# Gated linear attention with a gated feed-forward layer: PSUM banks split two for the late attention units and three in turn for gate, value and unit outputs, gating ranked first in the planner from step 15, last output banks finished one after another

## The chip, the cores and the metric

The kernel runs on one core of a Trainium2 chip. The metric is device time in microseconds (us). Three runs of the kernel before gave 572.51, 572.71 and 572.79 us, median 572.71. A profile of one more execution gives every number of the trace that follows.

The core's engines have queues of their own and run them in order: TensorE (PE: matmuls, with its weight loads shown as PEld), VectorE (DVE), ScalarE (ACT), GpSimd (POOL) and SyncE (SP, which here only issues DMAs). They wait for each other through semaphores.

## The reference

```python
def _attn_ref(q, k, v, alpha):                    # (4, 8, 768, 48) each
    B, H, S, D = q.shape
    state = np.zeros((B, H, D, D), dtype=np.float32)
    y = np.zeros_like(q)
    for t in range(S):
        state = alpha[:, :, t, :, None] * state + np.einsum('bhd,bhe->bhde', k[:, :, t], v[:, :, t])
        y[:, :, t] = np.einsum('bhd,bhde->bhe', q[:, :, t], state)
    return y.astype(np.float32)

def _moe_ref(x, w_gate, w_val, w_out):            # x (3072, 384), d_ff 1536
    gate = 1.0 / (1.0 + np.exp(-(x @ w_gate)))
    val = x @ w_val
    return (gate * val @ w_out).astype(np.float32)
```

The attention's output, laid out as 3072 tokens of 384 channels, is the x of the feed-forward layer. The weights are fp32, and the gate's weights are drawn larger by a factor of 6.92.

## The kernel before

**The feed-forward part: 72 steps.** The tokens are cut into six groups of 512, and d_ff into 12 blocks of 128. Step s works on group s // 12 and block s % 12. Every fp32 factor is split into a high and a low part, and a product is formed from three of the four partial products (`PAIRS`), so a step has 27 matmuls of 128x512: nine for the gate into bank `pg` and nine for the value into bank `pv` (`products`, L221), and nine into the three output banks `po0` to `po2` (`back`, L607). Between them stands the gating: the sigmoid `sg` on ACT (L594), `pv` times `sg` in place on DVE (L596), its high part `hh` cast on ACT (L598), and its low part `hl` by a subtraction on DVE (L599). Two of the three output partial products need `hh` alone, the third needs `hl`. `sg` has one buffer, `hh` and `hl` two. After a group's last step the three output banks are copied to SBUF (L620 on DVE, L622 on ACT) and sent out by SP (L623).

**The attention part: 24 units**, four for each group, each for two heads and 512 tokens. Units 0 to 7 come first (`unit`); units 8 to 23 (`late`) are spread over the steps, one in three, so that unit u's outputs follow steps 13, 16, ... 58. On the way a late unit goes through: loads of its rows (L498 to L509), a backward scan `G` on DVE (L366), the keys times `G` on POOL (L373), a forward scan `F` on DVE (L370), the queries times `F` on DVE (L514, two halves into the buffer `A`), four transposes on PE (L385) and their copy `kn` on ACT (L389), sixteen-fold small matmuls for the scores (L525) and for the state increments (L532), eight recurrent state updates `st` on DVE (L551), four masked copies of the scores on DVE (L538), the states times the decay on POOL (`vs`, L556), and the outputs on PE (L568). The outputs are split into `yt`, the high part on ACT (L396) and the low part on DVE (L397), and SP moves them into x (L405), from which the next group's steps read.

**The eight PSUM banks** are: three called `at` (`r_at`), one `pg`, one `pv`, three `po`. A late unit takes the three `at` banks for its transposes (`pk`) and for scores and increments (`pas[0]`, `pas[1]`). Its outputs go into the bank `pg`, the one that every step's gate uses too.

**What sets the order.** Nothing is issued where it stands in the code. Each piece is handed to `Plan.add` with its engine, an estimate of its duration, a key (the step at which it is due) and what it reads and writes. `Plan.order` first works out for each piece how late it may end (`latest`, from its key and from its users), then plays the engines forward with the estimated durations, and each time takes, of the pieces of an engine that could begin, the one with the smallest `latest`. The queues that result are fixed in the program: each engine then runs its queue in order, whatever the true durations are. Parts that share a PSUM bank or an SBUF buffer wait for each other through semaphores.

**The end.** The last step's pieces are keyed half a step earlier. After the plan, each engine loads a flag (`found`) and branches past a fallback loop (`general`) that the inputs here do not take.

The lines that set the places named here:

```python
r_bank = Ring([*r_at.tiles, *r_po.tiles, *r_pg.tiles])          # units 0 to 3
(pkn, pk), *pas = r_at.next(), r_at.next(), r_at.next()         # L517, late units
pyn, py = r_pg.tiles[0]                                         # L562, a late unit's outputs
n = min((n for n in ns if begin[n] <= t + 1e-9), key=lambda n: (latest[n], n))   # L108
```

Of the kernel before, what the change touches and what calls it, by code (L numbers as in the profile page):

```python
# [17 lines left out]
P = 128  # L18
# [30 lines left out]
class Plan:  # L49
# [14 lines left out]
    def add(self, engine, time, key, fn, reads=(), writes=(), port=False, fixed=False):  # L64
# [12 lines left out]
        self.parts.append((engine, time, key, fn, deps, port or engine == "gpsimd", fixed))  # L77

    def order(self):
# [14 lines left out]
        for n in reversed(range(len(self.parts))):  # L94
# [4 lines left out]
            latest[n] = by if key is None else key * self.STEP if self.parts[n][6] and key > NF + 2 else min(by, key * self.STEP)  # L99
        begun, memory, port, busy = [None] * len(self.parts), 0.0, 0.0, {}  # L100
        for _ in self.parts:
            best = None
            for e, ns in waiting.items():
# [4 lines left out]
                n = min((n for n in ns if begin[n] <= t + 1e-9), key=lambda n: (latest[n], n))  # L108
# [88 lines left out]
def gla_then_glu(ctx: ExitStack, tc: tile.TileContext, q, k, v, alpha, rows, vc, vh, weights_in, out):  # L197
# [11 lines left out]
    found = nc.values_load(within[0:1, 0:1], min_val=0, max_val=1)  # L209
# [15 lines left out]
def chunked(ctx, tc, rows, vc, vh, weights_in, out, const, ident, flags, weights, within):  # L225
# [70 lines left out]
    r_bank = Ring([*r_at.tiles, *r_po.tiles, *r_pg.tiles])  # L296
    ob = [(f"raw{i // 2}", raws[i // 2][1].rearrange("p a b -> p (a b)").bitcast(F32)[:, i % 2 * T:(i % 2 + 1) * T]) for i in range(NM)]
# [196 lines left out]
    def late(u, g, p, t):  # L494
# [22 lines left out]
        (pkn, pk), *pas = r_at.next(), r_at.next(), r_at.next()  # L517
# [44 lines left out]
        pyn, py = r_pg.tiles[0]  # L562
# [20 lines left out]
    def step(s):  # L583
        g, f = divmod(s, NF)
        got = {}
        for nm, r, dt in (("g", r_pg, 0.0), ("v", r_pv, 0.33)):
            pn, pt = r.next()
            got[nm] = (pn, pt)
            for tiles in ([range(NK - 1), range(NK - 1, NK)] if s < 2 else [range(NK)]):
                plan.add("tensor", (MM * 3 * len(tiles), 1.0), s + dt, lambda nm=nm, pt=pt, tiles=tiles: products(  # L590
                    nc, pt[:, 0:T], lambda a, i: weights.part(nm, a, f)[:, i], lambda b, i: xin(g)[:, i, b, :], tiles),
                    [*weight(nm, f), *(x for x in xparts[g] if x[1] in tiles)], [pn])
        (sgn, sg), (hhn, hh), (hln, hl) = r_sg.next(), r_hh.next(), r_hl.next()
        plan.add("scalar", act(T), None, lambda: nc.scalar.activation(out=sg, in_=got["g"][1][:, 0:T], func=AF.Sigmoid), [got["g"][0]], [sgn])  # L594
        pvn, pv = got["v"][0], got["v"][1][:, 0:T]
        plan.add("vector", vec(T), None, lambda: nc.vector.tensor_tensor(out=pv, in0=pv, in1=sg, op=ALU.mult), [sgn], [pvn])  # L596
        last = s == NG * NF - 1
        plan.add("scalar", act(T), None, lambda: nc.scalar.copy(out=hh, in_=pv), [pvn], [hhn])  # L598
        plan.add("vector", vec(T), None, lambda: nc.vector.tensor_tensor(out=hl, in0=pv, in1=hh, op=ALU.subtract), [pvn, hhn], [hln])  # L599
# [224 lines left out]
```

## Time and profile before

The profiled execution took 573.94 us; from its first to its last instruction is a span of 572.2 us, and the mean granted TensorE clock is 0.991. It lies 1.2 us above the median of the runs.

| stretch (us) | what runs | PE busy | DVE busy | PE clock |
|---|---|---|---|---|
| 28.6 to 57.2 | first units, first steps | 24.05 of 28.60 | 24.12 | 0.88 |
| 178.62 to 463.03 | thirteen periods of three steps and one late unit | 280.57 of 284.41 | 172.27 | 1.00 |
| 483 to 560 | steps alone | 77.00 of 77.00 | 17.44 | 1.00 |

Over the span PE is busy for 96%, DVE for 60%, ACT for 32% and POOL for 18%. A row of the timeline gives start, duration, engine, line, operation, output <- inputs, shape and count, and in brackets how long the engine was idle before it and what ended that. Matmuls overlap: a 128x512 matmul is shown with some 0.40 us, while the next one begins 0.23 us after it, so the time that PE loses is read from start to start rather than from the busy share.

### The profile page before, as it was taken

The page shows a single profiled execution, that of the slowest core. Times are in us where ns is not written, and L with a number is a line of the kernel's source. Part 1 is how long each engine was busy: PE and PEld are TensorE (multiplying, and loading weights), DVE is VectorE, ACT ScalarE, POOL GpSimd, SP SyncE. Part 2 cuts the span into 40 slices and gives each one's busy share as a digit, 9 for nine tenths or more (in the row PEclk, how much of TensorE's full clock was granted, in tenths as well). Part 3 has the DMA queues.
Part 4 walks back from the last instruction along what each step waited for, and adds up shares of the span by engine and source line. Part 5 has one row for each costly group of instructions (what it writes and reads, how often), then busy time and mean ns, then how long its engine had stood idle before and what let it go on. Part 6 is the DMA issues. An engine that isn't in the chain of part 4 may idle for free.

```text
span 572.2 us, 10280 instructions
## 1 busy us (share of the span) xinstructions
PE 550.2 (96%) x4150; PEld 434.2 (76%) x4150; DVE 344.9 (60%) x648; ACT 183.4 (32%) x331; POOL 102.2 (18%) x133
## 2 busy tenths in 40 slices
PE   8979999989999999999999999999999999999995
PEld 4657887767787787877877877877877878888783
DVE  7797989899848457467466476476475242311221
ACT  1557667653222222322222321321321222212111
POOL 7531212132202112112022022022021010000000
PEclk9988999999999999999999999999999999999998
DMA  8764765634414214314123224034131011100001
GB/s 327 239 189 152 256 209 177 196 122 124 136 32 113 75 37 111 125 42 113 52 61 111 85 82 112 13 100 112 58 109 49 13 29 29 56 0 1 1 0 62
DMA packets 21833, 55.93 MB, mean 98 GB/s; under 512 B 3472, under 2 KB 8592, under 8 KB 21776
## 3 DMA queue, kind: packets, MB, share of 16 engines
q1 hardware_dynamic: 21776, 55.17, 31.7%
q8 instruction: 35, 0.57, 0.4%
q14 instruction: 22, 0.18, 0.1%
HBM read 41.01 MB, written 4.72 MB: 80 GB/s over the span
## 4 chain that ended last, share of the span: by engine, by line
PE 76%; DVE 15%; issue 3%; DMA 2%; POOL 1%; SPq 1%; ACT 0%; DVEq 0%; POOLq 0%; ACTq 0%
PE pg L221 26%; PE pv L221 25%; PE po L607 17%; DVE st L551 6%; DVE A L538 4%; DVE yt L397 2%; PE at L525 2%; PE at L385 1%; DMA x<-yt 1%; PE pv L579 1%; PE at L532 1%; PE at L437 1%; POOL in L425 1%; DVE w L340 1%; POOL in L373 1%
## 5 line engine op out<-in xcount | busy, mean ns | idle before, releaser
L221 PE MATMUL pg<-x,w 128*128 128x512 f32 x648 | 163.6, 396 | 7.0 <-DVE yt L397 4.3
L221 PE MATMUL pv<-x,w 128*128 128x512 f32 x648 | 161.8, 394 | 1.0 <-DVE hl L599 1.0
L596 DVE TENSOR_TENSOR pv<-pv,sg 128x512 f32<-128x512 f32 x72 | 50.3, 699 | 175.5 <-PE pv L221 175.5
L221 PEld LDWEIGHTS pg<-x,w 128*128 128x128 f32 x648 | 120.2, 188 | 40.4 <-DVE yt L397 10.9
L221 PEld LDWEIGHTS pv<-x,w 128*128 128x128 f32 x648 | 120.6, 188 | 26.7 <-DVE hl L599 1.5
L607 PE MATMUL po<-hh,w 128*128 128x512 f32 x432 | 116.2, 401 | 1.2 <-ACT hh L598 1.2
L594 ACT ACTIVATE sg<-pg 128x512 f32<-128x512 f32 x72 | 43.1, 599 | 175.8 <-PE pg L221 175.7
L607 PEld LDWEIGHTS po<-hh,w 128*128 128x128 f32 x432 | 79.4, 188 | 20.6 <-ACT hh L598 1.5
L598 ACT CAST hh<-pv 128x512 fp32r<-128x512 f32 x72 | 42.2, 587 | 121.3 <-DVE pv L596 121.2
L556 POOL TENSOR_TENSOR vs<-st,dec 64x384 f32<-64x384 f32 x32 | 26.8, 839 | 226.1 <-DVE st L551 224.9
L607 PE MATMUL po<-hl,w 128*128 128x512 f32 x216 | 63.3, 399 | 0.0
L599 DVE TENSOR_TENSOR hl<-pv,hh 128x512 fp32r<-128x512 f32 x72 | 49.2, 683 | 20.5 <-ACT hh L598 20.4
L373 POOL TENSOR_TENSOR in<-in,G 128x512 f32<-128x512 f32 x22 | 33.9, 1541 | 86.6 <-DVE G L366 45.2
L607 PEld LDWEIGHTS po<-hl,w 128*128 128x128 f32 x216 | 40.4, 188 | 9.7 <-issue 0.2
L551 DVE SCALAR_TENSOR_TENSOR st<-st,dec,at 128x48 f32<-128x48 f32 x128 | 33.9, 265 | 9.4 <-PE at L532 4.1
L514 DVE TENSOR_TENSOR A<-A,F 64x512 f32<-64x512 f32 x32 | 33.4, 1043 | 0.5
L366 DVE TENSOR_TENSOR_SCAN G<-in,d1g 128x512 f32<-128x512 f32 x22 | 27.8, 1262 | 2.0 <-DMA in<-in_rows_dram 2.0
L370 DVE TENSOR_TENSOR_SCAN F<-in,d1f 128x512 f32<-128x512 f32 x22 | 28.7, 1304 | 0.0
L538 DVE TENSOR_TENSOR A<-at,mask 64x256 f32<-64x256 f32 x64 | 27.0, 422 | 1.1
L378 ACT ACTIVATE F<-F 128x512 f32<-128x512 f32 x23 | 14.5, 631 | 22.7 <-DVE A L514 16.9
L336 DVE SCALAR_TENSOR_TENSOR raw<-raw 128x576 uint32<-128x576 uint32 (+1 forms) x28 | 20.5, 751 | 0.8 <-ACT raw L333 0.8
L389 ACT COPY kn<-at 128x512 f32<-128x512 f32 x22 | 12.9, 584 | 15.5 <-PE at L385 15.5
(132 smaller groups left out, 400.1 us busy)
## 6 DMA issues: line engine op xcount, KB each, us to landing
in<-in_rows_dram SPq DMA_DIRECT2D x16, 516.5 KB, 3.9
raw<-in_w_dram SPq DMA_DIRECT2D x12, 576.0 KB, 4.9
x<-yt SPq DMA_DIRECT2D x35, 192.0 KB, 3.4
first_w<-in_w_dram SPq DMA_DIRECT2D x10, 576.0 KB, 4.5
out_dram<-raw SPq DMA_DIRECT2D x18, 256.0 KB, 2.4
v<-in_vc_dram SPq DMA_DIRECT2D x22, 192.0 KB, 4.8
A<-in_rows_dram SPq DMA_DIRECT2D x32, 128.0 KB, 4.1
in<-in_rows_dram SPq DMA_DIRECT2D x4, 772.5 KB, 5.2
```

The lines of the kernel that those rows point to most:

```text
L221: nc.tensor.matmul(out=dst, lhsT=lhs(a, i), rhs=rhs(b, i), start=(n == 0 and i == 0), stop=(n == len(todo) - 1 and i == NK - 1))
L366: plan.add("vector", scan(n), t["G"], lambda: nc.vector.tensor_tensor_scan(out=G[:, ::-1], data0=az[:, n:0:-1], data1=d1g[size], initial=0 ...
L370: plan.add("vector", scan(n), after(t["G"], 0.01), lambda: nc.vector.tensor_tensor_scan(out=F, data0=az[:, 0:n], data1=d1f, initial=0.0, o ...
L373: plan.add("gpsimd", pool_(n), t["kt"], lambda: nc.gpsimd.tensor_tensor(out=kT, in0=kT, in1=G, op=ALU.mult), [gn, (inn, "r")], [(inn, "k")])
L514: plan.add("vector", vec(T), t["q"], lambda j=j: nc.vector.tensor_tensor(out=A[own[j], j], in0=A[own[j], j], in1=F[own[j]], op=ALU.mult), ...
L538: plan.add("vector", vec(T // 2), t["mask"], lambda pa=pa, j=j, i=i: nc.vector.tensor_tensor(out=A[other[j], j].rearrange("p (c i t) -> p ...
L551: nc.vector.scalar_tensor_tensor(out=st[:, c + 1, :], in0=st[:, c, :], scalar=dec[:, c:c + 1], in1=pas[c % 2][1][:, T // 2 + c // 2 * D:T ...
L594: plan.add("scalar", act(T), None, lambda: nc.scalar.activation(out=sg, in_=got["g"][1][:, 0:T], func=AF.Sigmoid), [got["g"][0]], [sgn])
L596: plan.add("vector", vec(T), None, lambda: nc.vector.tensor_tensor(out=pv, in0=pv, in1=sg, op=ALU.mult), [sgn], [pvn])
L598: plan.add("scalar", act(T), None, lambda: nc.scalar.copy(out=hh, in_=pv), [pvn], [hhn])
L599: plan.add("vector", vec(T), None, lambda: nc.vector.tensor_tensor(out=hl, in0=pv, in1=hh, op=ALU.subtract), [pvn, hhn], [hln])
L607: nc.tensor.matmul(out=pso_now[m][1][:, 0:T], lhsT=weights.part("o", b, f)[:, m * P:(m + 1) * P], rhs=h[a][:, 0:T], start=(f == 0 and i == ...
```

## The change

It has five parts:

1. **Banks.** Two rings are added over banks that exist already. Late units take their three banks from `r_two` (`at0`, `at1`), so that `pk` and `pas[1]` are one bank. From step 12 the gate, the value and a late unit's outputs take the next bank of `r_three` (`pg`, `pv`, `at2`), in the order in which the code names them.
2. **Rank.** From step 15 the four gating pieces (`sg`, the product in place, `hh`, `hl`) carry `soon`, which puts them ahead of every other piece of their engine that could begin at the same time. Their `latest` is unchanged.
3. **The last step's output matmuls** are keyed bank by bank (all three products of `po0`, then of `po1`, then of `po2`) instead of product by product.
4. **The last output bank** `po2` is copied in two halves, columns 0 to 255 on ACT and 256 to 511 on DVE; the banks before it and all earlier groups are copied whole as before.
5. The flag `found` is loaded inside the `with` that holds the fast path's pools instead of just behind it.

```diff
-    def add(self, engine, time, key, fn, reads=(), writes=(), port=False, fixed=False):
+    def add(self, engine, time, key, fn, reads=(), writes=(), port=False, fixed=False, soon=False):
...
+        rank = [t - 1000.0 if p[7] else t for t, p in zip(latest, self.parts)]
...
-                n = min((n for n in ns if begin[n] <= t + 1e-9), key=lambda n: (latest[n], n))
+                n = min((n for n in ns if begin[n] <= t + 1e-9), key=lambda n: (rank[n], n))
...
-    found = nc.values_load(within[0:1, 0:1], min_val=0, max_val=1)
+        found = nc.values_load(within[0:1, 0:1], min_val=0, max_val=1)
...
+    r_two, r_three = Ring(r_at.tiles[:2]), Ring([*r_pg.tiles, *r_pv.tiles, r_at.tiles[2]])
...
-        (pkn, pk), *pas = r_at.next(), r_at.next(), r_at.next()
+        (pkn, pk), *pas = r_two.next(), r_two.next(), r_two.next()
...
-        pyn, py = r_pg.tiles[0]
+        pyn, py = r_three.next()
...
-            pn, pt = r.next()
+            pn, pt = (r_three if g else r).next()
...
+        soon = s > NF + 2
...
-        plan.add("scalar", act(T), None, lambda: nc.scalar.activation(out=sg, in_=got["g"][1][:, 0:T], func=AF.Sigmoid), [got["g"][0]], [sgn])
+        plan.add("scalar", act(T), None, lambda: nc.scalar.activation(out=sg, in_=got["g"][1][:, 0:T], func=AF.Sigmoid), [got["g"][0]], [sgn], soon=soon)
...
-                plan.add("tensor", (MM * len(some), 1.0), s + 1 + 0.66 + 0.01 * m + 0.1 * some[0] - (0.5 if last else 0), lambda m=m, some=some: back(m, some),
+                plan.add("tensor", (MM * len(some), 1.0), s + 1 + 0.66 + (0.1 * m + 0.01 * some[0] - 0.5 if last else 0.01 * m + 0.1 * some[0]), lambda m=m, some=some: back(m, some),
...
+                for half in range(2):
+                    cs = slice(half * T // 2, (half + 1) * T // 2) if last and m == NM - 1 else slice(0, T)
+                    n = cs.stop - cs.start
+                    if n == T and half != m % 2:
+                        continue
+                    if half:
+                        plan.add("vector", vec(n), s + 1.9, lambda pt=pt, to=to, cs=cs: nc.vector.tensor_copy(out=to[:, cs], in_=pt[:, cs]), [pn], [("ob", m, half), *over])
+                    else:
+                        plan.add("scalar", act(n), s + 1.9, lambda pt=pt, to=to, cs=cs: nc.scalar.copy(out=to[:, cs], in_=pt[:, cs]), [pn], [("ob", m, half), *over])
```

The other three gating pieces get `soon=soon` in the same way. Lines move by three to nine: L607 becomes L611, L568 L571, L385 L388, L397 L400, L599 L603, L620 L629.

PE's queue is the same up to step 10. In the steady part it reads so behind the outputs of the late unit that follow step 22, before (the number behind a name is the buffer's: `at2_119` is the third `at` bank, `x1_653` the next group's x, `w10` the weights of block 10):

```order
L568 MATMUL pg0_120<-A1_87,vs1_89 48x64 x16
L607 MATMUL po0_122<-hh1_114,w9_1037 128x512 x2
...
L607 MATMUL po0_122<-hl1_116,w9_1037 128x512
...
L607 MATMUL po0_122<-hh0_113,w10_1127 128x512 x2
...
L221 MATMUL pg0_120<-x0_111,w11_1250 128x512 x9
L221 MATMUL pv0_121<-x0_111,w11_1250 128x512 x9
L607 MATMUL po0_122<-hl0_115,w10_1127 128x512
...
L221 MATMUL pg0_120<-x1_653,w0_429 128x512 x9
L385 MATMUL at0_117<-ident_58,in1_79 128x128 x4
L221 MATMUL pv0_121<-x1_653,w0_429 128x512 x9
```

And with the change (of the three `po` banks only the first one's rows are shown, here and above):

```order
L571 MATMUL at2_119<-A1_87,vs1_89 48x64 x16
L611 MATMUL po0_122<-hh1_114,w9_1037 128x512 x2
...
L611 MATMUL po0_122<-hl1_116,w9_1037 128x512
...
L222 MATMUL pg0_120<-x0_111,w11_1250 128x512 x9
L222 MATMUL pv0_121<-x0_111,w11_1250 128x512 x9
L611 MATMUL po0_122<-hh0_113,w10_1127 128x512 x2
...
L611 MATMUL po0_122<-hl0_115,w10_1127 128x512
...
L222 MATMUL at2_119<-x1_653,w0_429 128x512 x9
L222 MATMUL pg0_120<-x1_653,w0_429 128x512 x9
L388 MATMUL at1_118<-ident_58,in1_79 128x128 x4
```

The outputs go into a bank that the next gate does not use; the six `hh` matmuls of block 10 that stood ahead of that gate now stand behind its value product, and the transposes stand behind a value product instead of between gate and value. The next group's first gate comes 36 matmuls after the outputs (9 output, 18 gate and value, 9 output) where it came 36 after them as well (15, 18 and 3).

DVE's queue at the same place, from the last state update on, before:

```order
L551 SCALAR_TENSOR_TENSOR st1_108<-st1_108,dec1_97,at2_119 128x48
L538 TENSOR_TENSOR A1_87<-at1_118,mask64_104 64x4x64
L538 TENSOR_TENSOR A1_87<-at2_119,mask64_104 64x4x64
...
L397 TENSOR_TENSOR yt0_85<-pg0_120,yt0_85 128x512
L599 TENSOR_TENSOR hl1_116<-pv0_121,hh1_114 128x512
L366 SCALAR_TENSOR_TENSOR G1_91<-in1_79,d1g64_102 128x512
L514 TENSOR_TENSOR A0_86<-A0_86,F0_92 64x512 x2
...
L596 TENSOR_TENSOR pv0_121<-pv0_121,sg0_112 128x512
```

And with the change (the two masked copies stand twice in each queue, the small pieces of 8 columns are left out):

```order
L554 SCALAR_TENSOR_TENSOR st1_108<-st1_108,dec1_97,at1_118 128x48
L603 TENSOR_TENSOR hl1_116<-pv0_121,hh1_114 128x512
L541 TENSOR_TENSOR A1_87<-at0_117,mask64_104 64x4x64
L541 TENSOR_TENSOR A1_87<-at1_118,mask64_104 64x4x64
...
L400 TENSOR_TENSOR yt0_85<-at2_119,yt0_85 128x512
L369 SCALAR_TENSOR_TENSOR G1_91<-in1_79,d1g64_102 128x512
L517 TENSOR_TENSOR A0_86<-A0_86,F0_92 64x512
L600 TENSOR_TENSOR pv0_121<-pv0_121,sg0_112 128x512
L517 TENSOR_TENSOR A0_86<-A0_86,F0_92 64x512
```

`hl` moves ahead of the masked copies and of `yt`; the next step's product goes between the two halves of the queries' multiplication.

Where the change to the rank begins, PE's queue of steps 10 to 13 differs by more than this. Behind the six output matmuls of block 10 it has, before and then with the change (rows of the other `po` banks left out):

```order
L385 MATMUL at0_117<-ident_58,in1_79 128x128 x4
L221 MATMUL pv0_121<-x0_111,w11_1250 128x512 x9
L221 MATMUL pg0_120<-x1_653,w0_429 128x512 x9
L607 MATMUL po0_122<-hl0_115,w10_1127 128x512
...
L607 MATMUL po0_122<-hh1_114,w11_1250 128x512 x2
L221 MATMUL pg0_120<-x1_653,w1_496 128x512 x9
L221 MATMUL pv0_121<-x1_653,w0_429 128x512 x9
```

```order
L222 MATMUL pv0_121<-x0_111,w11_1250 128x512 x9
L222 MATMUL pg0_120<-x1_653,w0_429 128x512 x9
L611 MATMUL po0_122<-hl0_115,w10_1127 128x512
...
L388 MATMUL at1_118<-ident_58,in1_79 128x128 x4
L611 MATMUL po0_122<-hh1_114,w11_1250 128x512 x2
L222 MATMUL pv0_121<-x1_653,w0_429 128x512 x9
```

The transposes move from before block 11's value product to behind the next gate. At the very end, DVE's half of the last bank waits in the built program for ACT's half of the same bank; the two do not run side by side.

More of the change, by code (lines that the diff above doesn't have):

```diff
@@ L76, in add @@
         deps.discard(n)
-        self.parts.append((engine, time, key, fn, deps, port or engine == "gpsimd", fixed))
+        self.parts.append((engine, time, key, fn, deps, port or engine == "gpsimd", fixed, soon))
     def order(self):
@@ L592, in step @@
                     [*weight(nm, f), *(x for x in xparts[g] if x[1] in tiles)], [pn])
+        soon = s > NF + 2
         (sgn, sg), (hhn, hh), (hln, hl) = r_sg.next(), r_hh.next(), r_hl.next()
-        plan.add("scalar", act(T), None, lambda: nc.scalar.activation(out=sg, in_=got["g"][1][:, 0:T], func=AF.Sigmoid), [got["g"][0]], [sgn])
+        plan.add("scalar", act(T), None, lambda: nc.scalar.activation(out=sg, in_=got["g"][1][:, 0:T], func=AF.Sigmoid), [got["g"][0]], [sgn], soon=soon)
         pvn, pv = got["v"][0], got["v"][1][:, 0:T]
-        plan.add("vector", vec(T), None, lambda: nc.vector.tensor_tensor(out=pv, in0=pv, in1=sg, op=ALU.mult), [sgn], [pvn])
+        plan.add("vector", vec(T), None, lambda: nc.vector.tensor_tensor(out=pv, in0=pv, in1=sg, op=ALU.mult), [sgn], [pvn], soon=soon)
         last = s == NG * NF - 1
-        plan.add("scalar", act(T), None, lambda: nc.scalar.copy(out=hh, in_=pv), [pvn], [hhn])
-        plan.add("vector", vec(T), None, lambda: nc.vector.tensor_tensor(out=hl, in0=pv, in1=hh, op=ALU.subtract), [pvn, hhn], [hln])
+        plan.add("scalar", act(T), None, lambda: nc.scalar.copy(out=hh, in_=pv), [pvn], [hhn], soon=soon)
+        plan.add("vector", vec(T), None, lambda: nc.vector.tensor_tensor(out=hl, in0=pv, in1=hh, op=ALU.subtract), [pvn, hhn], [hln], soon=soon)
         h = (hh, hl)
@@ L618, in step @@
                 over = [(on, "u"), (on, "l")] if g == 0 else []
-                if m % 2:
-                    plan.add("vector", vec(T), s + 1.9, lambda pt=pt, to=to: nc.vector.tensor_copy(out=to, in_=pt[:, 0:T]), [pn], [("ob", m), *over])
-                else:
-                    plan.add("scalar", act(T), s + 1.9, lambda pt=pt, to=to: nc.scalar.copy(out=to, in_=pt[:, 0:T]), [pn], [("ob", m), *over])
+                for half in range(2):
[7 more added lines that the diff above has]
+                        plan.add("scalar", act(n), s + 1.9, lambda pt=pt, to=to, cs=cs: nc.scalar.copy(out=to[:, cs], in_=pt[:, cs]), [pn], [("ob", m, half), *over])
                 plan.add("sync", (0.475, 1.0), s + 1.9, lambda to=to, m=m: nc.sync.dma_start(
-                    out=out[m * P:(m + 1) * P, g * T:(g + 1) * T], in_=to), [("ob", m)])
+                    out=out[m * P:(m + 1) * P, g * T:(g + 1) * T], in_=to), [("ob", m, 0), ("ob", m, 1)])
     pso = []
```

## The prediction

> **What bounds the kernel now.** I read the page's chain first, then the table of who waited for whom, then the timeline of one period of three steps in the steady part.
>
> ```profile
> PE 76%; DVE 15%; issue 3%; DMA 2%; POOL 1%; SPq 1%; ACT 0%; DVEq 0%; POOLq 0%; ACTq 0%
> L221 PE MATMUL pg<-x,w 128*128 128x512 f32 x648 | 163.6, 396 | 7.0 <-DVE yt L397 4.3
> PE pg L221 <- DVE yt L397: 4.3, 15, 0.6
> ```
>
> The chain that ended last is mostly PE. PE's largest wait on another engine, in total, is that of the gate's matmuls for `yt`: fifteen times, 4.3 us. One period shows what stands behind it (PE alone):
>
> ```profile
> 222.33 2.34 PE L221 MATMUL pg<-x,w 128*128 128x512 f32 x9 [0.27 <-DVE yt L397]
> 224.51 2.20 PE L221 MATMUL pv<-x,w 128*128 128x512 f32 x9
> 227.25 2.21 PE L221 MATMUL pg<-x,w 128*128 128x512 f32 x9
> 229.31 0.60 PE L385 MATMUL at<-ident,in 128*128 128x128 f32 x4
> 229.66 2.32 PE L221 MATMUL pv<-x,w 128*128 128x512 f32 x9
> 231.82 1.57 PE L607 MATMUL po<-hh,w 128*128 128x512 f32 x6
> 233.23 0.87 PE L607 MATMUL po<-hl,w 128*128 128x512 f32 x3
> 233.93 2.24 PE L221 MATMUL pg<-x,w 128*128 128x512 f32 x9
> 236.01 2.20 PE L221 MATMUL pv<-x,w 128*128 128x512 f32 x9
> ...
> 239.13 1.10 PE L568 MATMUL pg<-A,vs 128*48 128x64 f32 x32
> 240.16 1.67 PE L607 MATMUL po<-hh,w 128*128 128x512 f32 x6
> 242.37 1.56 PE L607 MATMUL po<-hh,w 128*128 128x512 f32 x6
> 244.20 2.11 PE L221 MATMUL pg<-x,w 128*128 128x512 f32 x8 [0.28 <-DVE yt L397]
> ```
>
> The unit's outputs go into `pg` at 239.13, and the next gate, at 244.20, may not write `pg` before ACT and DVE have split the outputs. The printed 0.28 understates this. Three matmuls begin at 233.23 and the next one at 233.93, while their row lasts 0.87: a row's end lies 0.17 behind the start of what follows. So the gate lost 0.28 + 0.17 = 0.45 us, and then a restart: nine gate matmuls take 2.18 from start to start at 222.33 but 2.08 at 233.93. That is 0.55 us a unit. DVE is late with `yt` because of its queue:
>
> ```profile
> 239.23 2.43 DVE L551 SCALAR_TENSOR_TENSOR st<-st,dec,at 128x48 f32<-128x48 f32 x8 [0.21 <-PE at L532]
> 241.70 1.73 DVE L538 TENSOR_TENSOR A<-at,mask 64x256 f32<-64x256 f32 x4
> 243.46 0.69 DVE L397 TENSOR_TENSOR yt<-pg,yt 128x512 fp32r<-128x512 f32 x1
> 244.06 0.68 DVE L599 TENSOR_TENSOR hl<-pv,hh 128x512 fp32r<-128x512 f32 x1
> 244.17 1.18 SPq L405 DMA_DIRECT2D x<-yt  x2
> 244.66 1.22 DVE L366 TENSOR_TENSOR_SCAN G<-in,d1g 128x512 f32<-128x512 f32 x1
> ```
>
> Apart from that stall PE has nothing to wait for here, and a step without a unit runs at PE's own pace: 550.48 - 544.25 = 6.23 us for 27 matmuls.
>
> ```profile
> 544.25 2.24 PE L221 MATMUL pg<-x,w 128*128 128x512 f32 x9
> 550.48 2.24 PE L221 MATMUL pg<-x,w 128*128 128x512 f32 x9
> ```
>
> **Part 1, the banks in the steady part.** With three banks in turn, the products around a unit's outputs fall so: gate A, value B, outputs C, gate A, value B, gate C. I count from E, the start of the first output matmul behind the unit's outputs (240.16 above). PE's queue then has nine output matmuls (2.2 with their restart), gate A at E+2.2, value B at E+4.2, nine output matmuls, gate C at E+8.4. Gate A needs the sigmoid of the gate before, long done. Value B needs `hl` of the value before: DVE's queue puts it right behind the state updates, which end at 241.66, E+1.5, so `hl` ends at E+2.2, 2.0 us early. Gate C needs `yt`, which `hl` moves back by 0.6 to 244.15 + 0.6 = E+4.6, 3.8 us early. The stall of 0.55 has no successor of its own.
>
> How often: 15 waits, of which one belongs to the start-up part (the row at 155.66 below, 0.19). The other 14 come to 4.3 - 0.19 = 4.1 printed, plus 14 x 0.17 = 2.4, plus 14 restarts of 0.10 = 1.4: **7.9 us less**. The transposes cost the same at their new place as at the old one: 229.66 - 229.31 = 0.35, and a restart of 0.1 (231.82 - 229.66 = 2.16 against 2.08 for nine matmuls). I cost the sharing of a bank by `pk` and `pas[1]` at nothing: between the transposes at 229.31 and the outputs at 239.13, just ahead of which the scores stand, ACT has over 8 us to copy `pk` out; without this cover it would be one ACT copy, 0.6 a unit. What covers the rest is DVE's queue; if `hl` came more than 2.0 us later, value B would wait for it.
>
> **The group's edge.** Three times, behind the units of steps 22, 34 and 46, gate C is the next group's first and reads the x that this unit's DMAs bring; its third matmul reads the last of them, at E+8.4+0.46 = E+8.9.
>
> ```profile
> x<-yt SPq DMA_DIRECT2D x35, 192.0 KB, 3.4
> ```
>
> The DMAs are issued behind `yt`, the second one 0.59 (half of 1.18) behind the first: E+4.6+0.6 = E+5.2, and landed at E+8.6. Before, the stall itself gave 0.55 more room and `hl` stood behind. So 0 to 0.5 a time; I take 0.1 in all, and 1.5 as the bad end.
>
> **Part 2, the rank at the start-up.** Steps 10 to 14 reorder, and there it costs.
>
> ```profile
> 134.23 1.57 PE L607 MATMUL po<-hh,w 128*128 128x512 f32 x6
> 135.64 0.60 PE L385 MATMUL at<-ident,in 128*128 128x128 f32 x4
> 136.49 0.68 DVE L599 TENSOR_TENSOR hl<-pv,hh 128x512 fp32r<-128x512 f32 x1
> 137.22 2.34 PE L221 MATMUL pv<-x,w 128*128 128x512 f32 x9 [0.98 <-DVE hl L599]
> 142.67 0.69 DVE L599 TENSOR_TENSOR hl<-pv,hh 128x512 fp32r<-128x512 f32 x1
> 150.59 2.33 PE L221 MATMUL pv<-x,w 128*128 128x512 f32 x9
> 155.66 2.37 PE L221 MATMUL pg<-x,w 128*128 128x512 f32 x9 [0.19 <-DVE yt L397]
> ```
>
> Block 11's value product still uses `pv` (the new ring begins with step 12), and still waits for an `hl` whose place in DVE's queue hasn't changed, so it begins at 137.2 as before. The transposes stood inside this wait and now come behind the next gate, uncovered: 0.45. The value product of step 12 no longer has a second gate ahead of it: it arrives at 137.22 + 2.18 + 2.08 (value, gate) + 0.70 + 0.45 + 0.46 (three output matmuls, transposes, two more) = 143.1 and finds the `hl` that ends at 142.67 + 0.69 = 143.36: 0.3 and a restart, 0.4. In step 13 the outputs now precede the scores and increments, and `yt` the state updates. Before, the increments ended where the value product of step 13 begins, at 150.59; now this is 0.9 later (0.45 + 0.4), 151.5. Behind it DVE has `yt` 0.69, the state updates 2.43, the masked copies 1.73, and the product, one half of the queries' multiplication and `hl`, some 0.7 each: 158.4. The value product of step 14, which now shares its bank with that of step 13, arrives at 151.5 + 2.2 + 2.1 + 2.1 = 157.9 and waits 0.5 and a restart, 0.6. Off goes the wait at 155.66, 0.19 + 0.17 + 0.10 = 0.46. Sum 0.45 + 0.4 + 0.6 - 0.46 = **1.0 more**; bounds 0 (only the transposes lose their cover, and the wait that goes pays for it) and 2.2 (each of these estimates twice as bad).
>
> **Parts 3 and 4, the end.**
>
> ```profile
> 562.95 1.56 PE L607 MATMUL po<-hh,w 128*128 128x512 f32 x6
> 564.35 0.86 PE L607 MATMUL po<-hl,w 128*128 128x512 f32 x3
> 564.77 1.07 ACT L622 COPY raw<-po 128x512 f32<-128x512 f32 x2 [2.35 <-PE po L607]
> 565.38 1.68 SPq L623 DMA_DIRECT2D out_dram<-raw  x3
> L538 DVE TENSOR_TENSOR A<-at,mask 64x256 f32<-64x256 f32 x64 | 27.0, 422 | 1.1
> ```
>
> Before, a bank's copy begins 0.42 behind the start of its last matmul (564.77 - 564.35), and SP's three issues of 0.56 run on to 567.06. Bank by bank, the last matmuls begin at 563.42, 564.12 and 564.82. The third copy begins at 565.24; its halves run one after the other, ACT's some 0.35 (between half of 0.535 and all of it), DVE's 0.42 by the nearest row of 256 columns, so it ends at 566.1 and SP's last issue at 566.55: **0.5 less**. One whole copy on ACT would end at 565.78; the halves give 0.3 back. Bounds: 0, and 0.9 if they ran side by side. Part 5 moves no row of any queue: nothing.
>
> **The sum.** -7.9 + 0.1 + 1.0 - 0.5 = -7.3. The profiled execution, 573.94 us, would come to 566.6; it lies 1.23 above the median of the runs, 572.71, so the forecast is 572.71 - 7.3 = **565.4 us**.
>
> **The rivals.** Two stretches serve several of them (busy us of PE, PEld, DVE, ACT and POOL, then granted clock, DMA share and GB/s):
>
> ```profile
> 28.60:57.20 28.60, 24.05 (x196) 18.73 (x193) 24.12 (x47) 17.89 (x30) 6.17 (x8) 0.88 0.57 170
> 178.62:463.03 284.41, 280.57 (x2353) 225.22 (x2353) 172.27 (x338) 73.00 (x138) 49.62 (x59) 1.00 0.26 75
> ```
>
> *The gain comes whole:* the start-up costs nothing and the end brings 0.9: 572.71 - 7.9 - 0.9 + 0.1 = 564.0. For it: in the steady part DVE is busy for 172 of 284 us, so its delay can be worked off. Against it: PE, not DVE, is what the uncovered transposes burden.
>
> *The wait moves to x:* gate C at the groups' edges waits 0.5 each time and more where a DMA lands late, 565.4 + 1.4 = 566.8. For it: E+8.6 against E+8.9. Against it: only the third matmul reads that part.
>
> *The printed wait is all there is:* PE's row ends are modelled, and were the 0.17 and 0.10 not lost time, 14 units would give 4.1: 565.4 + 3.8 = 569.2. Against it: the starts themselves differ.
>
> *The change doesn't free the value's bank in time (slower):* the outputs take a third of the ring, so value B comes back to its bank after three products, and `hl` of the value before must be done by E+4.2. If DVE held `hl` behind the masked copies, `yt` and the next scan, as it does today except for the scan, it would end at E+2.2 + 1.73 + 0.69 + 1.22 = E+5.8: a wait of 1.6 + 0.1 in place of 0.55, 14 x 1.15 = 16 more, 572.71 + 16 = 589. It decides where `hl` comes 2.55 later than I have it. Against it: the queue is fixed with `hl` ahead of all three.
>
> *The clock (slower):* PE hops through more banks, idles briefly more often, and loses clock.
>
> Where PE idled for 16% the clock was 0.88; at that clock the steady 284 us would take 39 us more, 604. Against it: there the clock is 1.00 with all fourteen stalls, and the change takes idle time away. The Trainium skill ("TensorE: Matmul & The Clock Gate", section "A second HAM failure mode: psum-queue depth-cycling") says that cycling through PSUM banks each iteration left PE idle so often, for moments, that its clock swung between half and full. By that rule this rival would hold; this trace, at 1.00 while the banks alternate, doesn't bear it out.
>
> **How the numbers follow.** Forecast 0.58, whole gain 0.17, x 0.14, printed wait 0.06, `hl` 0.04, clock 0.01. The forecast's own bounds are 564.0 to 567.9 (1.0 less or 1.2 more at the start-up, 0.4 less or 0.5 more at the end, 1.4 more at the edges, not all at once), which take in the first two rivals too. 0.2% (1.1 us) is about what a measurement of this kernel can tell from no change. Faster than that are all but the last two cases; I leave 0.01 for no difference and 0.05 for slower.
>
> **What would show it.** Right: the wait of `pg` for `yt` gone from the table; a period of 21.3 in place of 21.87 us; some PE waits for `hl` between 137 and 160 us; DVE's half copy behind ACT's at the end. Wrong: PE waits for `hl` or for x in each period, a period no shorter, or a clock below 1.00 in the steady part.

## The result, and the profile after

The changed kernel takes 565.96 us (median of 565.53, 565.76, 566.16 and 569.32) where the kernel before, beside it, takes 572.75: a ratio of 0.989, 95% interval 0.9868 to 0.9912. In a later series it took 565.69 against 572.91, ratio 0.9864 (0.984 to 0.9887). So it is 6.8 to 7.2 us faster, and the forecast of 565.4 lies within 0.6 us. The profiled execution took 565.76 us, with a span of 564.0.

From the page of the changed kernel, the chain that ended last and the gate's group (busy, mean ns of one, idle time before it):

```profile
PE 87%; DVE 7%; DMA 2%; issue 2%; POOL 1%; ACT 1%; SPq 0%; DVEq 0%
...
L222 PE MATMUL pg<-x,w 128*128 128x512 f32 x477 | 119.9, 395 | 4.2 <-DMA x<-yt 4.0
```

And from its table of who waited for whom, PE's lines (total, times, longest) for x and `hl`:

```profile
PE pg L222 <- DMA x<-yt: 4.0, 2, 2.8
...
PE pv L222 <- DVE hl L603: 1.9, 2, 1.7
```

The wait of the gate for `yt` is gone from the table, and the chain has lost the pieces of DVE that led up to it (15% to 7%). What is left are waits of the first 160 us; the two for x fall before 45 us. The gate's group counts fewer matmuls because its work is now spread over three banks.

One period, PE first and then DVE, from the timeline:

```profile
237.75 1.67 PE L611 MATMUL po<-hh,w 128*128 128x512 f32 x6
239.25 0.86 PE L611 MATMUL po<-hl,w 128*128 128x512 f32 x3
239.95 2.24 PE L222 MATMUL pg<-x,w 128*128 128x512 f32 x9
242.03 2.20 PE L222 MATMUL pv<-x,w 128*128 128x512 f32 x9
244.07 1.57 PE L611 MATMUL po<-hh,w 128*128 128x512 f32 x6
245.48 0.87 PE L611 MATMUL po<-hl,w 128*128 128x512 f32 x3
246.19 2.24 PE L222 MATMUL at<-x,w 128*128 128x512 f32 x9
```

```profile
236.82 2.43 DVE L554 SCALAR_TENSOR_TENSOR st<-st,dec,at 128x48 f32<-128x48 f32 x8 [0.21 <-PE at L535]
239.17 0.68 DVE L603 TENSOR_TENSOR hl<-pv,hh 128x512 fp32r<-128x512 f32 x1
239.88 1.73 DVE L541 TENSOR_TENSOR A<-at,mask 64x256 f32<-64x256 f32 x4
241.64 0.69 DVE L400 TENSOR_TENSOR yt<-at,yt 128x512 fp32r<-128x512 f32 x1
```

E is 237.75. Gate A starts at E+2.20, value B at E+4.28, gate C at E+8.44; `hl` ends at 239.17 + 0.68 = E+2.10 and `yt` at E+4.58. The forecast had 2.2, 4.2, 8.4, 2.2 and 4.6. No row of PE carries a bracket: nothing waits.

**By stages.** Whole spans are a poor measure here, since they differ by more than a microsecond from run to run. I cut the trace at three rows of PE that every kernel of this study has: unit 7's products of the transposed rows, unit 10's scores and unit 23's scores. Before, and then after:

```profile
117.24 1.16 PE L437 MATMUL at<-in 48*128 48x128 f32 x16 [1.08 <-POOL in L425]
...
172.56 0.64 PE L525 MATMUL at<-A,in 48*64 48x64 f32 x28
...
457.00 0.69 PE L525 MATMUL at<-A,in 48*64 48x64 f32 x32
```

```profile
115.55 1.16 PE L440 MATMUL at<-in 48*128 48x128 f32 x16 [1.07 <-POOL in L428]
...
171.52 0.69 PE L528 MATMUL at<-A,in 48*64 48x64 f32 x31
...
449.41 0.69 PE L528 MATMUL at<-A,in 48*64 48x64 f32 x32
```

The table holds the differences of such starts (us), for the runs of the experiments too, so that they can be read against each other:

| kernel | start to unit 7's products | start-up, to unit 10's scores | 13 periods, to unit 23's scores | to the start of the last matmul | to the end |
|---|---|---|---|---|---|
| before | 117.24 | 55.31 | 284.44 | 107.81 | 7.41 |
| after | 115.55 | 55.98 | 277.89 | 107.34 | 7.28 |
| e1, banks alone | 115.94 | 55.96 | 277.91 | 107.34 | 8.13 |
| e2, rank alone | 116.43 | 55.33 | 283.72 | 107.82 | 7.32 |
| e3, end alone | 116.35 | 55.30 | 284.45 | 107.80 | 7.30 |
| e4, own bank | 116.33 | 59.37 | 277.65 | 107.34 | 7.44 |
| e5, after again | 116.40 | 55.94 | 277.59 | 107.34 | 7.25 |
| e6, own bank later | 116.72 | 55.40 | 277.85 | 107.34 | 7.84 |
| e7, rank from step 9 | 115.20 | 56.02 | 277.60 | 107.34 | 8.83 |
| e8, `hl` late | 115.98 | 55.93 | 283.93 | 107.82 | 6.95 |
| e9, own bank and end | 115.99 | 55.35 | 277.82 | 107.34 | 7.21 |
| e10, q on POOL | 117.31 | 55.26 | 277.61 | 107.34 | 8.00 |
| e11, whole last copy | 117.99 | 55.62 | 277.79 | 107.34 | 7.37 |

Of the 8.2 us between the two profiled spans, 1.7 lie in the first stage, ahead of the first row of PE that the change moves. Over all runs that stage takes 115.2 to 118.0 us, before's 117.24 being among the long ones, so this part is no effect of the change. The rest is +0.67 in the start-up, -6.55 in the thirteen periods, -0.47 to the start of the last matmul, and -0.13 at the end: 6.5 us. (A unit's outputs come behind the next unit's scores, so the last of the 14 stalls, at 463.03, belongs to unit 22 and lies behind unit 23's scores.) In the second trace of the changed kernel, e5, the same four stages come to 6.85 us less.

### The profile page after: what moved, and what is told of

It is laid out like the page before. It is cut to its first block, busy times and chain, and to the rows that moved or that the text cites. A ratio compares the mean times of both kernels' runs of the same rounds, so it can differ in the third digit from the quotient of the medians.

```text
span 564.0 us, 10267 instructions
## 1 busy us (share of the span) xinstructions
PE 544.8 (97%) x4150; PEld 433.4 (77%) x4150; DVE 333.8 (59%) x649; ACT 183.5 (33%) x331; POOL 101.5 (18%) x133
## 2 busy tenths in 40 slices
DMA packets 21833, 55.93 MB, mean 99 GB/s; under 512 B 3472, under 2 KB 8592, under 8 KB 21776
## 4 chain that ended last, share of the span: by engine, by line
PE 87%; DVE 7%; DMA 2%; issue 2%; POOL 1%; ACT 1%; SPq 0%; DVEq 0%
PE po L611 26%; PE pg L222 18%; PE pv L222 18%; PE at L222 14%; PE at L528 2%; PE at L388 1%; DMA x<-yt 1%; PE pv L582 1%; PE pv L571 1%; PE pg L571 1%; PE at L571 1%; PE at L535 1%; PE at L440 1%; DVE st L554 1%; DVE raw L339 1%
## 5 line engine op out<-in xcount | busy, mean ns | idle before, releaser
L222 PE MATMUL pg<-x,w 128*128 128x512 f32 x477 | 119.9, 395 | 4.2 <-DMA x<-yt 4.0
L611 PE MATMUL po<-hh,w 128*128 128x512 f32 x432 | 117.5, 404 | 0.6 <-ACT hh L602 0.6
L222 PE MATMUL pv<-x,w 128*128 128x512 f32 x459 | 115.0, 394 | 1.9 <-DVE hl L603 1.9
L222 PEld LDWEIGHTS pg<-x,w 128*128 128x128 f32 x477 | 89.3, 189 | 25.5 <-issue 3.5
L222 PEld LDWEIGHTS pv<-x,w 128*128 128x128 f32 x459 | 86.1, 189 | 22.4 <-DVE hl L603 2.8
L611 PEld LDWEIGHTS po<-hh,w 128*128 128x128 f32 x432 | 78.4, 188 | 18.6 <-ACT hh L602 0.9
L222 PE MATMUL at<-x,w 128*128 128x512 f32 x360 | 89.2, 392 | 0.0
L222 PEld LDWEIGHTS at<-x,w 128*128 128x128 f32 x360 | 67.4, 188 | 15.3 <-issue 0.3
L611 PE MATMUL po<-hl,w 128*128 128x512 f32 x216 | 63.5, 398 | 0.0
L600 DVE TENSOR_TENSOR pv<-pv,sg 128x512 f32<-128x512 f32 x32 | 22.3, 696 | 62.8 <-PE pv L222 61.4
L600 DVE TENSOR_TENSOR pg<-pg,sg 128x512 f32<-128x512 f32 x21 | 14.7, 699 | 58.7 <-PE pg L222 58.5
L611 PEld LDWEIGHTS po<-hl,w 128*128 128x128 f32 x216 | 40.4, 188 | 9.9 <-issue 0.2
L598 ACT ACTIVATE sg<-pg 128x512 f32<-128x512 f32 x32 | 19.2, 599 | 57.2 <-PE pg L222 57.0
L602 ACT CAST hh<-pv 128x512 fp32r<-128x512 f32 x32 | 18.8, 587 | 49.3 <-DVE pv L600 49.3
```

The lines of the kernel that those rows point to most:

```text
L222: nc.tensor.matmul(out=dst, lhsT=lhs(a, i), rhs=rhs(b, i), start=(n == 0 and i == 0), stop=(n == len(todo) - 1 and i == NK - 1))
L611: nc.tensor.matmul(out=pso_now[m][1][:, 0:T], lhsT=weights.part("o", b, f)[:, m * P:(m + 1) * P], rhs=h[a][:, 0:T], start=(f == 0 and i == ...
```

## The experiments

The kernels that leave out a part of the change still load the flag `found` where part 5 puts it. That this is worth nothing can be seen from e2 and e3, which have it and take as long as the kernel before.

**e1, the banks alone** (the kernel before with these lines):

```diff
-        (pkn, pk), *pas = r_at.next(), r_at.next(), r_at.next()
+        (pkn, pk), *pas = r_two.next(), r_two.next(), r_two.next()
-        pyn, py = r_pg.tiles[0]
+        pyn, py = r_three.next()
-            pn, pt = r.next()
+            pn, pt = (r_three if g else r).next()
```

> The kernel before with part 1 alone (the two rings of banks); rank, last step and halves as before. My theory: the banks carry the gain. PE's queue of this kernel is that of the changed one up to the last step, the start-up with its moved transposes included, so the +1.0 I gave to the rank there comes with the banks. hl now stands behind the masked copies and ends at E+2.2+1.7 = E+3.9, 0.3 ahead of value B at E+4.2, so nothing waits for it: 572.7 - 7.9 + 0.1 + 1.0 = 565.9 us, period 21.3 us, no wait of the gate for yt. Rival 1 (the rank is what keeps hl in time): value B waits for hl in each of 14 periods, 0.3 to 1.7 each, 570 to 589 us. Rival 2 (the start-up cost belongs to the rank): 564.9 us, and the block-11 value product is followed by covered transposes.

Measured: 567.05 us against 573.08, ratio 0.9891 (0.9866 to 0.9917), as good as the ratio of the whole change. The timeline of one period, two rows of PE and one of DVE:

```profile
238.08 1.67 PE L611 MATMUL po<-hh,w 128*128 128x512 f32 x6
...
242.37 2.20 PE L222 MATMUL pv<-x,w 128*128 128x512 f32 x9
...
241.37 0.69 DVE L603 TENSOR_TENSOR hl<-pv,hh 128x512 fp32r<-128x512 f32 x1
```

`hl` ends at E+3.98 and value B begins at E+4.29, without a wait: the margin of 0.3 is there. The start-up takes 55.96 us, as in the changed kernel. So the banks bring the gain, and the start-up's cost comes with them too; rivals 1 and 2 fall.

One period is an exception: the last of the thirteen, which takes 21.55 us here. In it DVE pauses for 0.46 us behind the first of the eight state updates, `hl` ends at 433.90 + 0.69 = 434.59, and value B begins right there and needs 2.18 us to the next start instead of 2.08 (two rows of DVE and two of PE):

```profile
430.06 2.07 DVE L554 SCALAR_TENSOR_TENSOR st<-st,dec,at 128x48 f32<-128x48 f32 x7 [0.46 <-DVE st L554]
...
433.90 0.69 DVE L603 TENSOR_TENSOR hl<-pv,hh 128x512 fp32r<-128x512 f32 x1
...
434.64 2.34 PE L222 MATMUL pv<-x,w 128*128 128x512 f32 x9
436.82 1.57 PE L611 MATMUL po<-hh,w 128*128 128x512 f32 x6
```

Nine of the thirteen traces have this pause; its cause is open. Before, it made one stall longer and that period 22.15 us:

```profile
441.24 2.33 PE L221 MATMUL pg<-x,w 128*128 128x512 f32 x9 [0.61 <-DVE yt L397]
```

In the changed kernel, where the rank puts `hl` further ahead, the same period takes 21.33 us with the pause. So the rank is worth 0.2 us here, and nothing in the other periods.

**e2, the rank alone** (`soon` and `rank` as in the change, the banks of before):

> The kernel before with part 2 alone (the gating ranked first); banks and end as before. In its PE queue the value product of the step behind a unit's outputs comes ahead of that step's gate, so the gate, which still shares its bank with the outputs, comes at E+4.3 and yt, put back by hl, ends at E+4.6. My theory: a wait of about 0.3 and a restart stays in each unit, 0.4 for 0.55, so the rank alone brings 14 x 0.15 = 2: 570.6 us (569 to 572.5), and the wait of the gate for yt stays in the table. Rival 1 (yt is only put back, and the gate stands where it stood): 14 x 0.6 more, 581 us. Rival 2 (the order alone hides yt): the wait is gone, 565 us, and the banks are not needed.

Measured: 572.42 us, ratio 0.9989 (0.9975 to 1.0003), at the edge of the range and short of 570.6. Two rows of PE and one of DVE:

```profile
241.45 2.30 PE L222 MATMUL pv<-x,w 128*128 128x512 f32 x9
243.89 2.35 PE L222 MATMUL pg<-x,w 128*128 128x512 f32 x9
...
243.15 0.69 DVE L400 TENSOR_TENSOR yt<-pg,yt 128x512 fp32r<-128x512 f32 x1
```

The value product has moved ahead of the gate, and still the gate waits for `yt`, which ends at 243.84. The value product takes 2.44 to the next start instead of 2.08, and the gate again 0.1 more for its restart: 0.47 a unit for 0.53 before. The table of waits prints 1.8 us of this, in eleven waits. Hiding it takes another bank, not another order. The start-up is 55.33 us, that of before: the rank does not move it.

**e3, the end alone** (the new keys of the last output matmuls and the halves of the last copy, the rest as before):

> The kernel before with parts 3 and 4 alone (last output banks finished one after another, last bank copied in halves). My theory: 0.5 less, 572.2 us; ACT's half and DVE's half of the last bank run one after the other (0.35 and 0.42), and from the start of the last output matmul to the end of SP's last issue it is 1.7 us. Rival 1 (what follows SP's last issue takes the gain back): 572.7 us, no difference. Rival 2 (the halves run side by side): 571.8 us.

Measured: 572.70 us, ratio 1.0006 (0.9989 to 1.0023): no difference, as rival 1 has it. What becomes of the half microsecond is told with e11.

**e4, a bank of their own for the outputs**, gate and value in `pg` and `pv` as before:

```diff
-        (pkn, pk), *pas = r_at.next(), r_at.next(), r_at.next()
+        (pkn, pk), *pas = r_two.next(), r_two.next(), r_two.next()
-        pyn, py = r_pg.tiles[0]
+        pyn, py = r_at.tiles[2]
```

> The kernel before with one bank set apart for a late unit's outputs (the third at bank) and two banks in turn for the rest of the unit; gate and value stay in pg and pv, no rank, old end. My theory: only the outputs' bank matters, the three in turn do not. PE's queue in the steady part is that of the changed kernel by name of work; hl ends at E+3.9 and value B, in the bank whose product hl reads, comes at E+4.2. So 572.7 - 7.9 = 564.8 us, and up to 1.0 more by the start-up, where the transposes stand elsewhere than in both kernels; period 21.3 us. Rival (gate and value need a third bank, since each value product waits for the hl two products earlier): a wait for hl in each period of 0.3 to 0.9, 568 to 577 us.

Measured: 569.53 us, ratio 0.9937 (0.9915 to 0.9958). That looks like the rival, but the stages say otherwise: the thirteen periods take 277.65 us, no more than with three banks in turn, and the loss is in the start-up, 59.37. Its rows of PE:

```profile
132.66 0.63 PE L388 MATMUL at<-ident,in 128*128 128x128 f32 x4 [1.78 <-POOL st L550]
...
136.13 1.66 PE L611 MATMUL po<-hh,w 128*128 128x512 f32 x6 [1.81 <-ACT hh L602]
...
141.01 2.34 PE L222 MATMUL pv<-x,w 128*128 128x512 f32 x9 [1.15 <-DVE hl L603]
```

With a bank free the plan brought unit 9's transposes and unit 8's outputs forward, into three waits: PE runs its queue in order, and what these pieces read was not ready. Whether the plan's estimates had it ready there, no run shows. My forecast allowed 1.0 for this; it was 4.1.

**e5 to e8** were run side by side. **e5** is the changed kernel again:

> The changed kernel once more, beside the next three on one chip. Ratio to the kernel before 0.989, some 566.5 us where the kernel before takes 573; from the last transposed products of unit 7 to the scores of unit 10 56.0 us (55.3 in the kernel before), from there to the scores of unit 23 277.9 us (284.4).

565.69 us, ratio 0.9864 (0.984 to 0.9887). Against e1 neither the time nor a whole stage tells the rank apart; only the one period named there does.

**e6, the own bank from unit 9 on:**

```diff
+        rr = r_two if u >= 9 else r_at
+        (pkn, pk), *pas = rr.next(), rr.next(), rr.next()
...
+        pyn, py = r_at.tiles[2] if u >= 9 else r_pg.tiles[0]
```

> The kernel before with one bank set apart for a late unit's outputs, as in e4, but from unit 9 on: unit 8 keeps its three banks and pg. No rank, old end. My theory: e4 lost its gain in the start-up alone, where the new bank let the plan bring unit 8's work forward into waits; this kernel's PE queue is that of the kernel before up to unit 9's outputs, so the start-up stays at 55.3 us (less 0.5 for unit 9's own wait for yt), and the steady part takes 277.8 us as in e4: 573.0 - 7.5 = 565.5 us, about 1 us under the changed kernel. Rival 1 (the start-up's cost comes back at unit 9): 567 to 569 us. Rival 2 (without the rank hl is late, its margin being 0.3): a wait of value B for hl in the periods, above 568 us.

Measured: 566.73 us, ratio 0.9882 (0.9856 to 0.9907); start-up 55.40, periods 277.85. The start-up's cost is gone and the steady gain is whole, so e4's loss was the start-up's. The 0.5 that I had counted for a wait in the start-up did not come: the wait there, 0.21 at 155.21, is behind the outputs of unit 8, which still share `pg`; unit 9's lies in the periods. Without the rank the last period takes 21.54 us, as in e1.

**e7, the rank from step 9** (e6 with the new end and `soon = s >= 9`):

> e6 with the new end and with the gating ranked first from step 9 instead of 15. In DVE's queue hl of step 10 then stands ahead of the last low parts of block 11's weights, 1.3 us of work, which puts it behind the masked copies. My theory: block 11's value product, which waits 1.0 to 1.7 us for this hl in the traces of before and after, waits 1.2 us less, and nothing else in the start-up is later by as much: 564.3 us, start-up 54.1 us. Rival (the weights of block 11, now 3.0 us later, or the next gate's x become the wait): start-up 55.3 us or more, 565.5 us or more.

Measured: 566.82 us, ratio 0.9891 (0.9871 to 0.991), start-up 56.02. Its table of waits has no `hl` any more, but this:

```profile
PE po L612 <- ACT hh L603: 2.8, 2, 1.5
```

Of these two waits one (1.33, at 109.00) lies ahead of the start-up stage. The other is new (PE, then DVE):

```profile
137.41 2.20 PE L222 MATMUL pv<-x,w 128*128 128x512 f32 x9
141.09 1.20 PE L612 MATMUL po<-hh,w 128*128 128x512 f32 x4 [1.48 <-ACT hh L603]
...
139.72 0.70 DVE L601 TENSOR_TENSOR pv<-pv,sg 128x512 f32<-128x512 f32 x1 [0.76 <-PE pv L222]
```

PE no longer waits for `hl`, but then for `hh`. DVE is not what is late here, it waits for PE itself: the plan has put the next gate, with a wait of 0.34 for x, ahead of block 11's value product, and what stands next in PE's queue needs the `hh` of that product. The rival holds in kind: other waits take the place.

**e8, `hl` late.** Only the rank of one piece differs from the changed kernel:

```diff
-        rank = [t - 1000.0 if p[7] else t for t, p in zip(latest, self.parts)]
+        rank = [t - 1000.0 * p[7] for t, p in zip(latest, self.parts)]
...
-[pvn, hhn], [hln], soon=soon)
+[pvn, hhn], [hln], soon=-0.005 if 16 <= s <= 58 and s % 3 == 1 else soon)
```

> The changed kernel, with hl of the step before a unit's outputs moved behind yt in DVE's queue (from the unit of step 16 on); PE's queue is the same row for row. This tests the rival in which hl comes too late for the next value product in its bank. My theory: hl ends at E+4.5 for value B's E+4.3, a wait of 0.25 and a restart of 0.1 in each of 15 units: 5 us more than the changed kernel, 571.5 us, period 21.7 us, and a wait of the value, gate or at bank for hl in each period. Rival (the next product begins without regard to it, or PE makes it up): 566.5 us, period 21.3 us.

Measured: 572.92 us, beside 565.69 of e5 and 572.91 of the kernel before (ratio 0.9998, 0.9985 to 1.0011). Three rows of one period, the last of DVE:

```profile
239.36 1.67 PE L611 MATMUL po<-hh,w 128*128 128x512 f32 x6
...
244.00 2.33 PE L222 MATMUL pv<-x,w 128*128 128x512 f32 x9 [0.19 <-DVE hl L603]
...
243.27 0.68 DVE L603 TENSOR_TENSOR hl<-pv,hh 128x512 fp32r<-128x512 f32 x1
```

`hl` ends at E+4.59, 2.49 later than in the changed kernel; value B begins at E+4.64 instead of E+4.28, and restarts. A period takes 6.34 / 13 = 0.49 more than in e5 (the prediction of this run had 0.35). So the rival in which `hl` comes too late is a real mechanism. The forecast put the point from which it decides at 2.55 later; 2.49 later the kernel is just as slow as before.

**e9 to e11** were run side by side again. **e9** is e6 with the change's rank and end:

> The changed kernel with a simpler set of banks: gate and value keep pg and pv, a late unit's outputs have the third at bank to themselves from unit 9 on, and unit 8 keeps its old banks; rank and new end as in the changed kernel. My theory: the start-up stays at the 55.4 us of e6 and the kernel before instead of 56.0, the steady part at 277.7 us, so it is 0.5 us faster than the changed kernel: ratio to the kernel before 0.986. Rival (three banks in turn spare a wait that I don't see, or the rank costs at the start-up once the banks are gone): ratio 0.988 or more.

Measured: 565.57 us against 572.82, ratio 0.9871 (0.9854 to 0.9887), start-up 55.35. By its stages it is 0.6 us better than the changed kernel in the start-up, as expected. The time can't tell them apart, and the ratio that I gave, 0.986, isn't shown.

**e10, unit 9's queries on POOL** (e9 with this):

```diff
+            qe = "gpsimd" if u in (9,) and j in (0, 1) else "vector"
+            plan.add(qe, pool_(T) if qe == "gpsimd" else vec(T), t["q"], lambda j=j, qe=qe: getattr(nc, qe).tensor_tensor(
```

> e9 with both halves of unit 9's multiplication of the queries by F on POOL instead of DVE (1.4 us of DVE's work between 139 and 142 us). My theory: between 110 and 145 us PE waits for a DVE that is busy all the time (24.5 of 25.4 us), so only work taken off it shortens the start-up: the value product of step 12 no longer waits for hl, 0.4 to 0.9 us less than e9, start-up 54.5 to 55.0 us. Rival (DVE and POOL slow each other where both multiply from SBUF, or PE's next wait takes its place): 55.4 us or more.

Measured: 565.70 us, ratio 0.9867 (0.9851 to 0.9884); start-up 55.26, 0.1 less than e9. The value product of step 12 has no printed wait:

```profile
142.82 2.35 PE L222 MATMUL pv<-x,w 128*128 128x512 f32 x9
```

This says little, though. `hl` ends at 142.76 here, so that the product begins right behind it, 0.13 later than the row ahead would let it. And in e9, with which this run is compared, that product stands behind its step's gate and has no wait to lose; a wait of this product for `hl`, 0.21 at 141.63, is in the changed kernel. The plan reordered the rows around it as well (the value product ahead of the gate, the outputs of unit 8 ahead of the scores), and 0.1 is all that was left of 0.4 to 0.9. That DVE is what bounds the start-up stays likely (it is busy for 24.49 of 25.42 us in e9's window from 110 us on) but this run didn't show it.

**e11, the last bank copied whole:**

```diff
-                    cs = slice(half * T // 2, (half + 1) * T // 2) if last and m == NM - 1 else slice(0, T)
+                    cs = slice(half * T // 2, (half + 1) * T // 2) if False else slice(0, T)
```

> The changed kernel with the last output bank copied whole by ACT instead of in two halves. My theory: ACT's copy ends 0.24 us earlier than DVE's half did (0.59 whole against 0.37, a gap of 0.03 and 0.42), so SP's last issue ends at 1.5 us behind the start of the last matmul instead of 1.75 and the last output packet lands 0.2 earlier; in the time it cannot be told from the changed kernel: ratio to the kernel before 0.986 to 0.989. Rival (the last transfer is bound by the two transfers ahead of it): the last packet lands where it did, 4.15 to 4.25 us behind the start of the last matmul.

Measured: 566.43 us, ratio 0.9878 (0.9861 to 0.9894). The end of the changed kernel (SP's three issues are one row), and then SP's row of e11, which likewise begins 0.36 ahead of the last matmul's start:

```profile
556.39 2.11 SPq L632 DMA_DIRECT2D out_dram<-raw  x3
...
556.75 0.39 PE L611 MATMUL po<-hl,w 128*128 128x512 f32 x1
557.18 0.37 ACT L631 COPY raw<-po 128x256 f32<-128x256 f32 x1 [0.81 <-PE po L611]
557.58 0.42 DVE L629 COPY raw<-po 128x256 f32<-128x256 f32 x1 [0.41 <-ACT raw L631]
```

```profile
558.39 2.55 SPq L632 DMA_DIRECT2D out_dram<-raw  x3
```

The halves run one after the other, and the last of them ends 1.25 us behind the start of the last matmul. The whole copy ends at 1.01, as expected. Yet SP's last issue ends at 2.19 there and not at 1.5: the issue ahead of it took 1.26 us, where it took 0.83 in the changed kernel (0.33 to 1.07 in the seven kernels with the halves). The last output packet ended at 4.35; in these seven kernels that is 3.93 to 4.32, on average 4.15, in the five with the old end 4.38 to 4.42, on average 4.40. So the rival is nearer: what was ready earlier at the copy did not get out earlier in this trace.

## Why the prediction was right, and where it wasn't

**The stall is real, and it is 0.53 us.** The period went from 21.86 (twelve of the thirteen, 21.83 to 21.87) to 21.33 us where nothing else changed, for 0.55 forecast. The 14 stalls gave 7.6 of the 7.9 forecast: 284.44 - 13 x 21.33 = 7.15 in the thirteen periods, the long one of 22.15 included, and 0.47 behind unit 22's outputs. The rival that only the printed wait is lost falls: 0.28 is printed, 0.53 came back.

**No stall took its place,** for the reason given: `hl` 2.0 and `yt` 3.8 us early, measured 2.18 and 3.86. e1 and e8 show the margin from both sides: `hl` at E+3.98 costs nothing, at E+4.59 everything. The forecast saw this margin as the gift of the rank; e1 shows that the steady part lives without it, by 0.3 us, but for the one period in which DVE pauses. The transposes cost what they did before, 0.35 and a restart, and no wait of `pk`'s bank appeared.

**The group's edge was mis-sized, by the time of a transfer.** From the timeline of the changed kernel, the first gate product behind an edge:

```profile
224.67 2.42 PE L222 MATMUL pv<-x,w 128*128 128x512 f32 x9
```

This is gate C, here in the bank `pv`. It takes 2.25 us to the start of what follows, where gate A above takes 242.03 - 239.95 = 2.08; the two longer steps stand ahead of its third and fourth matmul, 0.1 each. The last transfer of x was issued at E+5.2, as forecast (E is 216.23 here), but landed 3.66 us later, at 225.09, where the forecast took the median of 3.4; the third matmul was due at 225.13. The three periods with an edge take 21.51, 21.47 and 21.49 us instead of 21.33, together 0.48 where I took 0.1 (two other periods take 0.03 and 0.08 more, for a cause that I leave open). Before, they showed no such excess.

That x's last transfer is the cause was not tried by an edit of its own, but the thirteen traces bear it out at all their 39 edges. In the 27 where it lands 0.29 to 0.46 us behind the start of the first gate product, that product takes 2.12 to 2.29 us, by and large longer the later it lands. In the twelve of before, e2, e3 and e8, where it lands ahead of that start, the product takes 2.05 to 2.08.

**Part 2 failed in its cause, not in its size.** The prediction said that the rank reorders steps 10 to 14 and that it costs 1.0 there. e1 has the same start-up without the rank, and e2, with the rank, has that of before: the banks reorder the plan. The cost was 0.67. Its places were the foreseen ones, waits for `hl` and the uncovered transposes (all rows of the changed kernel):

```profile
135.42 2.35 PE L222 MATMUL pv<-x,w 128*128 128x512 f32 x9 [1.66 <-DVE hl L603]
...
140.35 0.60 PE L388 MATMUL at<-ident,in 128*128 128x128 f32 x4
...
141.63 2.34 PE L222 MATMUL pv<-x,w 128*128 128x512 f32 x9 [0.21 <-DVE hl L603]
...
156.34 2.36 PE L222 MATMUL pg<-x,w 128*128 128x512 f32 x9 [0.18 <-DVE hl L603]
```

**The end was mis-sized.** In these two traces SP's last issue does end 0.5 us earlier, 1.75 for 2.25 behind the start of the last matmul. But over the kernels it is 1.85 on average with the new end and its halves and 2.14 with the old end, 0.3 earlier, since SP's second issue took 0.33 to 1.07 where I had 0.56. The last packet ends 0.26 earlier, and the stage from the last matmul to the end is 0.13 shorter in the changed kernel; e3 measured no difference. I had stopped the sum at SP's last issue, and what follows the last packet, 2.9 to 4.9 us over the traces, differs more from run to run than the gain.

**The clock rival falls.** The changed kernel in the window in which the kernel before ran its thirteen periods (busy us of PE, PEld, DVE, ACT and POOL, then granted clock, DMA share and GB/s):

```profile
178.62:463.03 284.41, 284.41 (x2383) 231.45 (x2382) 161.99 (x339) 74.66 (x141) 49.42 (x59) 1.00 0.27 76
```

Gate and value go through three banks in turn, PE is busy throughout, and the clock is 1.00. The Trainium skill ("TensorE: Matmul & The Clock Gate", section "A second HAM failure mode: psum-queue depth-cycling") warns of a clock that swings where PSUM banks are cycled through and PE idles for moments in between; this trace shows neither the idle moments nor the swing.

In sum, from the two first traces: -7.6 for the stalls, +0.6 at the edges and in the two other periods, +0.7 in the start-up, -0.1 at the end, -6.5 in all (before rounding) for -7.3 forecast; e5's trace gives -6.85. The runs' medians show -6.8 and -7.2. Three terms promised 0.3 to 0.5 us too much each, and the start-up, whose cause was wrong, 0.3 too little. That the median lies within 0.6 us of the forecast is in part luck.

## What to carry to other kernels

When an engine waits once in each period for a buffer that another engine still reads, count from start to start what it loses (here 0.53 for 0.28 printed), and ask whether one buffer, moved, is enough: a bank of their own for the outputs gave all that three in turn for everything gave. Then check the place where the new scheme begins: a planner that gets freedom uses it there too, and e4 lost half of its gain to three waits within 10 us that the steady part never sees. Try each part of a bundle alone; here the new end brought nothing that can be measured, and the rank 0.2 us, in the one period in which DVE was late.

## What the runs showed that I had not expected

The first stage, with the same rows on PE in all kernels, takes 115.2 to 118.0 us, more than most parts of this change are worth. Stages cut at rows that all kernels have repeat within 0.3 us (start-up and periods of after and e5: 55.98 and 55.94, 277.89 and 277.59) and told apart what the runs' times could not.

From the start of the last matmul to the end it takes 6.95 to 8.83 us, whatever the end of the kernel is. The last output packet ends within 3.93 to 4.42 of them. In e7 the longest of these ends comes from DVE: its drain stands 2.65 us behind its event before it, while in the changed kernel it stands 0.11 behind. In e1, e6 and e11 it is 2.6 to 2.8 us as well; why is open.
